# Modulation rows 2, 3 and 4 as half rows in column strips, loaded back repeated over the partitions

## The chip, the cores and the metric

One core of one Trainium2 chip runs the kernel. The metric is the device time of one execution in microseconds (us), the median of several runs. Engines are named as in the profile: PE (TensorE, matmuls), DVE (VectorE), ACT (ScalarE), POOL (GpSimd), SP (SyncE, which here only issues DMAs).

## What is computed

One transformer block in bf16, forward and all gradients (batch 1, S = 2048 tokens, D = 1024, F = 3584):

```
mod = (silu(c) @ w_mod)              # c (1,1024), w_mod (1024, 6*1024)
sa, ca, ga, sb, cb, gb = six rows of mod, 1024 each
h = layernorm(x) * (1 + ca) + sa
x = x + ga * irfft2(rfft2(h) * (w_r + 1j*w_i))
h = layernorm(x) * (1 + cb) + sb
y = layernorm(h)
out = x + gb * (gelu(y @ w1 + b1) @ w2 + b2)
# outputs: out, and by vjp of grad_out the gradients of
# x, w_r, w_i, w1, b1, w2, b2, c, w_mod
```

The six rows of mod are numbered 0 (sa), 1 (ca), 2 (ga), 3 (sb), 4 (cb), 5 (gb). This case is about rows 2, 3 and 4.

## The kernel before

**The modulation.** Every elementwise operation with a row of mod needs that row on all 128 partitions. The kernel gets this from TensorE: `u_b` holds silu(c) as 8 blocks of 128 contraction rows, each column repeated over 128 columns. With a block of `u_b` as weights, a matmul gives the same row in all 128 partitions of its PSUM tile. `mod_block(r, h)` makes half h (512 columns) of row r: a weight tile `wblk` of w_mod (128x8x512, 1 MB, L245, on SP's queue, a ring of three tiles), 8 matmuls of 128x512 (L253) accumulating in a PSUM bank, a copy to the row's place (L256, on DVE or ACT as the scheduler picks), and for rows 1 and 4 an addition of one (L258, DVE). The places are `MOD_DST`: `ga_row` for row 2, `sb_row` for row 3 (half of the tile `sb_saf`), `opcb_row` for row 4 (1 + cb). Rows 1, 5 and 0 are made at the start; rows 2, 3 and 4 later, six blocks called `late_mods`.

**Fillers.** grad_out * gb times the transpose of W2 is needed only by the backward of the MLP. `ph_part(fc, js)` makes one of its 28 blocks of 128 rows: 4 x 8 matmuls (L684) into PSUM tiles `pp`, copies to `pho` or `phr` (L691, L694, ACT or DVE), and a store to `d_ph` on POOL's queue. `load_w2t(fg)` fetches the transposed weights for two blocks (L301, SP's queue, two slots `wt`). Six of these blocks (`PH_EARLY`) stand ahead of the spectral mixer, with three late modulation blocks behind fc=3 and three behind fc=5; the other 22 are dealt by the scheduler into places where PE has nothing else.

**The mixer and the MLP.** A loop over four pieces of 512 tokens (lines 709 to 722) normalizes x (`ln_mix`, `norm_act`: L451, L454, L461 on ACT and statistics on DVE), multiplies by 1 + ca, and folds it twice (`fold_tok`, `fold_d`, all additions at L173 on DVE) into `fbuf`; the last addition, of `saf`, completes a piece. The transforms are matmuls: `pu` (L472), `pcs` (L505), on DVE the products with the spectral weights (`R`), `pv` (L565), `po` (L630) with copies at L635. `consume_fwd(i)` takes a finished piece: unfolds it, stores it to `d_A`, multiplies by `ga_row`, adds x, normalizes, multiplies by `opcb_row`, adds `sb_row`, normalizes again, and stores to `d_n3`. Then `z_block(b, g0, g1)` runs the first MLP product (L802, PSUM `pz`) with a bias copy on ACT (L805), the square and two sigmoids on ACT (L807, L811, L813) and products on DVE; `bo_pass` runs the second product (L853).

**Order.** The kernel is written in a tile framework: a list scheduler puts the instructions of each engine in order before the run, `tc.high_priority()` puts an instruction ahead of others that are ready, and `tc.issue_after(x)` keeps it behind x. On the chip every engine and every DMA queue then works in that fixed order. So an edit in one place can move copies between ACT and DVE and fillers between stages elsewhere.

Of the kernel before, what the change touches and what calls it, by code (L numbers as in the profile page):

```python
# [11 lines left out]
BF16 = mybir.dt.bfloat16  # L12
I32 = mybir.dt.int32
ACT = mybir.ActivationFunctionType
ALU = mybir.AluOpType
AX = mybir.AxisListType

P = 128
S = 2048
D = 1024  # L20
# [4 lines left out]
KH = D // 2  # L25
# [10 lines left out]
def kernel(  # L36
# [24 lines left out]
    nc = tc.nc  # L61
# [5 lines left out]
    dram = ctx.enter_context(tc.tile_pool(name="dram", bufs=1, space=bass.MemoryType.DRAM))  # L67
# [5 lines left out]
    def ps_s(name):  # L73
        return psum.tile([P, 512], FP32, tag="s", name=name)
# [18 lines left out]
    opca_row, ga_row, opcb_row, gb_row = (rows4[:, r, :] for r in range(4))  # L93
# [19 lines left out]
    d_SI = dram.tile([P, 2, 4, 512], BF16, name="d_SI")  # L113
    d_E = dram.tile([P, 2, 8, 256], BF16, name="d_E")
    d_gmod = dram.tile([6 * D], BF16, name="d_gmod")
    d_ph_v = d_ph.rearrange("(fc p) s -> p fc s", p=P)
    d_hh_v = d_hh.rearrange("(fc p) s -> p fc s", p=P)
    d_gz_v = d_gz.rearrange("(fc p) s -> p fc s", p=P)
# [50 lines left out]
    def bcn(row, n):  # L169
        return bass.AP(tensor=row.tensor, offset=row.offset, ap=[row.ap[0], [0, n], row.ap[1]])  # L170

    def tt(out, a, b, op):
        return nc.vector.tensor_tensor(out=out, in0=a, in1=b, op=op)  # L173
# [56 lines left out]
    u_b = small.tile([P, NDC, P], BF16, name="u_b", tag="gmrow", bufs=1)  # L230
# [5 lines left out]
    MOD_DST = {0: sar[:, 0, 0, :], 1: opca_row, 2: ga_row, 3: sb_row, 4: opcb_row, 5: gb_row}  # L236
    wring = [0]

    def mod_tile():
        wring[0] += 1  # L240
        return reg.tile([P, NDC, KH], BF16, name="wblk", tag=PXT[3 + wring[0] % 3])

    def mod_load(r, h, wblk, eng):
        cb = 2 * r + h
        eng.dma_start(out=wblk, in_=w_mod[:, cb * KH:(cb + 1) * KH].rearrange("(j p) n -> p j n", p=P))  # L245

    def mod_block(r, h, wblk=None):
        if wblk is None:
            wblk = mod_tile()[:]
            mod_load(r, h, wblk, nc.sync)  # L250
        pm = ps_s("pm")
        for jc in range(NDC):
            nc.tensor.matmul(pm[:], lhsT=u_b[:, jc, :], rhs=wblk[:, jc, :], start=(jc == 0), stop=(jc == NDC - 1))  # L253
        dst = MOD_DST[r][:, h * KH:(h + 1) * KH]
        with tc.high_priority():
            nc.any.tensor_copy(out=dst, in_=pm[:])  # L256
        if r in (1, 4):
            nc.vector.tensor_scalar(out=dst, in0=dst, scalar1=1.0, scalar2=None, op0=ALU.add)  # L258

    def fold_d(dst, src, tmp):  # L260
        n = src.shape[1]
        fwd = src.rearrange("p c (b w) -> p c b w", w=512)[:, :, :, 0:256]
        rev = bass.AP(tensor=src.tensor, offset=src.offset + 1023, ap=[src.ap[0], [D, n], [-512, 2], [-1, 256]])
        tv = tmp.rearrange("p c (s b w) -> p c s b w", s=2, w=256)
        tt(tv[:, :, 0], fwd, rev, ALU.add)
        tt(tv[:, :, 1], fwd, rev, ALU.subtract)
        dv = dst.rearrange("p c (a b w) -> p c a b w", b=2, w=256)
        tt(dv[:, :, :, 0, :], tv[:, :, :, 0, :], tv[:, :, :, 1, :], ALU.add)
        return tt(dv[:, :, :, 1, :], tv[:, :, :, 0, :], tv[:, :, :, 1, :], ALU.subtract)
# [30 lines left out]
    def load_w2t(fg):  # L300
        w2t_in[0] = nc.sync.dma_start_transpose(out=wt[:, fg % 2], in_=B_w2[fg * 256:(fg + 1) * 256, :])  # L301
# [19 lines left out]
    for h in range(2):  # L321
        mod_block(1, h, wm[1, h][:])
# [17 lines left out]
    for j in range(4):  # L340
        for cch in range(NDC):
# [3 lines left out]
            if cch % 2 == 0:  # L345
                with tc.high_priority():
                    nc.vector.tensor_scalar(out=gBoT[j][:, cch, :], in0=pt[:], scalar1=gb_col[:, cch:cch + 1], scalar2=0.0,
                                            op0=ALU.mult, op1=ALU.add, accum_out=gu[:, j, cch:cch + 1])
# [68 lines left out]
    def ln_act(x4, row, i, jk):  # L417
        sv = small.tile([P, 4, 4], FP32, tag="lnsv")
        for q in range(4):
            nc.scalar.activation(out=jk[:, q, :], in_=x4[:, q, :], func=ACT.Identity, accum_out=sv[:, q, 0:1])  # L420
        nc.vector.tensor_scalar(out=sv[:, :, 1:2], in0=sv[:, :, 0:1], scalar1=-1.0 / D, scalar2=None, op0=ALU.mult)
        for q in range(4):
            nc.scalar.activation(out=jk[:, q, :], in_=x4[:, q, :], func=ACT.Square, bias=sv[:, q, 1:2], accum_out=sv[:, q, 2:3])
        ln_fin(sv[:, :, 2:3], sv[:, :, 1:2], sv[:, :, 3:4], 1.0 / D, row, i)
# [7 lines left out]
    def ln_dve(x4, row, i):  # L432
        st = small.tile([P, 4, 2, nc.vector.BN_STATS_DIM], FP32, tag="lnst", bufs=1)
        mv = small.tile([P, 4, 4], FP32, tag="lnmv")
        for q in range(4):
            for h in range(2):
                nc.vector.bn_stats(out=st[:, q, h, :], in_=x4[:, q, h * KH:(h + 1) * KH])
            nc.vector.bn_aggr(out=mv[:, q, 0:2], in_=st[:, q])
        nc.vector.tensor_scalar(out=mv[:, :, 2:3], in0=mv[:, :, 0:1], scalar1=-1.0, scalar2=None, op0=ALU.mult)
        ln_fin(mv[:, :, 1:2], mv[:, :, 2:3], mv[:, :, 3:4], 1.0, row, i)  # L440

    def ln_mix(x4, row, i, jk):
        st = small.tile([P, 4, 2, nc.vector.BN_STATS_DIM], FP32, tag="lnst", bufs=1)
        mv = small.tile([P, 4, 4], FP32, tag="lnmv")
        for q in range(2):
            for h in range(2):
                nc.vector.bn_stats(out=st[:, q, h, :], in_=x4[:, q, h * KH:(h + 1) * KH])
            nc.vector.bn_aggr(out=mv[:, q, 0:2], in_=st[:, q])
        nc.vector.tensor_scalar(out=mv[:, 0:2, 2:3], in0=mv[:, 0:2, 0:1], scalar1=-1.0, scalar2=None, op0=ALU.mult)
        for q in range(2, 4):  # L450
            nc.scalar.activation(out=jk[:, q, :], in_=x4[:, q, :], func=ACT.Identity, accum_out=mv[:, q, 0:1])  # L451
        nc.vector.tensor_scalar(out=mv[:, 2:4, 2:3], in0=mv[:, 2:4, 0:1], scalar1=-1.0 / D, scalar2=None, op0=ALU.mult)
        for q in range(2, 4):
            nc.scalar.activation(out=jk[:, q, :], in_=x4[:, q, :], func=ACT.Square, bias=mv[:, q, 2:3], accum_out=mv[:, q, 0:1])  # L454
        nc.vector.tensor_scalar(out=mv[:, 2:4, 1:2], in0=mv[:, 2:4, 0:1], scalar1=1.0 / D, scalar2=None, op0=ALU.mult)
        ln_fin(mv[:, :, 1:2], mv[:, :, 2:3], mv[:, :, 3:4], 1.0, row, i)
# [216 lines left out]
    last_pe = [None]  # L673
# [4 lines left out]
    def ph_part(fc, js):  # L678
        fg, k = fc // 2, fc % 2
        ph2 = phs[fc % 4]  # L680
        for j in js:
            pp = ps_f("pp")
            for cch in range(NDC):
                last_pe[0] = nc.tensor.matmul(pp[:], lhsT=wt[:, fg % 2, cch, k * P:(k + 1) * P], rhs=gBoT[j][:, cch, :],  # L684
                                              start=(cch == 0), stop=(cch == NDC - 1))
            q = (0, 2, 3, 1)[j]
            ov = ph2[:, :, q * P:(q + 1) * P]
            pv = pp[:, :].rearrange("p (i w) -> p i w", w=P)
            if j % 2 == 0:
                with tc.high_priority():  # L690
                    nc.any.tensor_copy(out=ov, in_=pv)  # L691
            else:
                with tc.high_priority():
                    nc.any.tensor_copy(out=ov, in_=bass.AP(tensor=pv.tensor, offset=pv.offset + 511, ap=[pv.ap[0], [-P, 4], [-1, P]]))  # L694
        if js[-1] == 3:
            nc.gpsimd.dma_start(out=d_ph[fc * P:(fc + 1) * P, :], in_=ph2.rearrange("p i w -> p (i w)"))

    PH_EARLY = 6
    late_mods = [(r, h) for r in (2, 3, 4) for h in range(2)]
    for fc in range(PH_EARLY):  # L700
        ph_part(fc, (0, 1, 2, 3))
        if fc % 2 == 1:
            load_w2t(fc // 2 + 2)
            if fc > 1:
                with tc.issue_after(last_pe[0].ins):
                    for r, h in late_mods[3 * (fc // 2 - 1):3 * (fc // 2)]:
                        mod_block(r, h)

    for i in range(4):
        x4, fb = x4s[i], fbuf[:, i]  # L710
        if i == 0:
            with tc.issue_after(u_in.ins):
                ln_dve(x4, 0, i)
        elif i > 0:
            ln_mix(x4, 0, i, fb)
        else:
            ln_act(x4, 0, i, fb)
        norm_act(fb, x4, 0, i)
        tt(fb, fb, bcn(opca_row, 4), ALU.mult)
        fold_tok(fb, x4)  # L720
        fold_d(fb, fb, x4[:])
        tt(fb[:, 0, :], fb[:, 0, :], saf, ALU.add)
    css = reg.tile([P, 2, 2, 2 * PW], BF16, name="cs01", tag="px0")
    nc.gpsimd.memset(css[:], 0.0)

# [206 lines left out]
    for g in range(7):  # L932
        wtile = reg.tile([P, 4, D], BF16, name=f"w1T_{g}", tag=W1T[g])
        for k in range(4):
            fc = g * 4 + k
# [162 lines left out]
    for b in range(NB):  # L1098
# [42 lines left out]
        for i in range(4):  # L1141
            t = 4 * b + i
            nc.vector.tensor_tensor_reduce(out=g2[:, i, :], in0=gn3[:, i, :], in1=opcb_row, scale=1.0, scalar=0.0,
                                           op0=ALU.mult, op1=ALU.add, accum_out=s2c[:, i:i + 1])
# [222 lines left out]
```

## Time and profile before

| | before |
|---|---|
| runs (us) | 1461.4, 1461.49, 1465.73; median 1461.49 |
| profiled execution (us) | 1459.13, span of the trace 1457.3 |
| granted PE clock, mean | 0.992 |
| busy | PE 96%, DVE 73%, ACT 52%, POOL 25% |
| L253, all 96 matmuls of the six rows | 27.9 us busy |

A line of a timeline has the start in us, the busy time in us, the engine, the source line, the operation with its tiles, the count of instructions taken together, and in brackets the idle time of the engine before it with what ended that. A group line has busy us and mean ns, then the idle time before the group's instructions and its main releaser. A matmul's own duration (379 ns) overlaps its neighbours'; the spacing, 0.217 us for 128x512, is what counts. In a line of windows the last three columns are the granted PE clock, the DMA share and GB/s.

### The profile page before, as it was taken

The numbers are of one execution on the slowest core, as the hardware profiler recorded it, in microseconds if no ns is written. First come the engines' busy times: TensorE is split into PE (matmuls) and PEld (weight loads), VectorE is DVE, ScalarE is ACT, GpSimd is POOL, SyncE is SP. The second block draws the span as 40 slices with busy tenths as digits, with TensorE's granted clock in tenths as the row PEclk, the third lists the DMA queues.
The fourth block names the chain that finished last, engine by engine and source line by source line (L and its number), as shares of the span: only waits on it lengthen the run. The fifth ranks groups of instructions, "written<-read, shape, count | busy, mean of one in ns | idle before, by whom it ended". The sixth has DMA issues, their size and how long they took to land. (4 is left out here: it accounts for less than half of the span.)

```text
span 1457.3 us, 18411 instructions
## 1 busy us (share of the span) xinstructions
PE 1396.5 (96%) x6835; PEld 649.0 (45%) x6835; DVE 1058.4 (73%) x1483; ACT 752.2 (52%) x1065; POOL 366.1 (25%) x441
## 2 busy tenths in 40 slices
PE   5889999999999999999999999999999999999997
PEld 2434545444444444444444444344444445444443
DVE  5884786898799787887520889898467678898650
ACT  4675555857887766665305574342622434344211
POOL 6520451211112122122211011021245441222432
PEclk8999999999999999999999999999999999999999
DMA  9962473899887877697998275297699987766991
GB/s 333 286 214 70 142 235 115 270 255 337 257 203 278 259 250 233 201 264 241 277 297 245 74 271 185 107 270 176 181 217 254 254 233 213 194 191 180 297 279 65
DMA packets 358367, 324.28 MB, mean 223 GB/s; under 512 B 209386, under 2 KB 301056, under 8 KB 358022
## 3 DMA queue, kind: packets, MB, share of 16 engines
q1 hardware_dynamic: 324166, 207.71, 52.7%
q0 software_dynamic: 34112, 115.41, 22.6%
q8 instruction: 53, 0.87, 0.2%
q14 instruction: 36, 0.29, 0.1%
HBM read 162.06 MB, written 111.20 MB: 188 GB/s over the span
## 5 line engine op out<-in xcount | busy, mean ns | idle before, releaser
L684 PE MATMUL pp<-gBoT,wt 128*128 128x512 bf16 x896 | 197.9, 380 | 4.5 <-DMA wt<-in_B_w_dram 2.6
L950 PE MATMUL pg<-w1T,gzr 128*128 128x512 bf16 x896 | 197.1, 381 | 0.2 <-ACT gn3b L961 0.2
L1266 PE MATMUL gw1acc<-gzh,n3n 128*128 128x512 bf16 x896 | 195.4, 379 | 1.3 <-DMA gzh<-d_gz 1.3
L684 PEld LDWEIGHTS <-wt 128*128 128x128 bf16 x896 | 87.7, 98 | 109.4 <-issue 4.2
L950 PEld LDWEIGHTS <-gzr 128*128 128x128 bf16 x896 | 87.3, 98 | 108.7 <-issue 6.6
L802 PEld LDWEIGHTS <-w 128*128 128x128 bf16 x896 | 87.3, 98 | 108.8 <-issue 4.7
L1266 PEld LDWEIGHTS <-n3n 128*128 128x128 bf16 x896 | 87.4, 98 | 106.1 <-issue 2.7
L802 PE MATMUL pz<-n3Tb,w 128*128 128x512 bf16 x448 | 99.2, 379 | 1.6 <-DVE w2sD L875 1.4
L802 PE MATMUL pz<-n3Ta,w 128*128 128x512 bf16 x448 | 98.7, 379 | 1.1 <-ACT gt L805 1.1
L1075 PE MATMUL gw2acc<-gB,hhsA 128*128 128x512 bf16 x448 | 98.5, 379 | 1.0 <-DMA hhsA<-d_hh 1.0
L853 PEld LDWEIGHTS <-hhA 128*128 128x128 bf16 x608 | 59.0, 98 | 71.7 <-issue 1.4
L805 ACT ACTIVATE gt<-pz,b_col 128x512 bf16<-128x512 f32 x112 | 72.5, 684 | 34.2 <-PE pz L802 32.8
L1270 ACT CAST gwo<-gw1acc 128x512 bf16<-128x512 f32 x50 | 29.1, 583 | 113.6 <-PE gw1acc L1266 99.0
L173 DVE TENSOR_TENSOR gt<-gt,gt 128x2048 bf16<-128x2048 bf16 x56 | 68.3, 1223 | 22.4 <-ACT gt L813 21.2
L1082 ACT CAST gwo<-gw2acc 128x512 bf16<-128x512 f32 x46 | 26.7, 583 | 109.9 <-PE gw2acc L1075 75.6
L811 ACT ACTIVATE gt<-gt 128x2048 bf16<-128x2048 bf16 x28 | 53.5, 1910 | 55.7 <-DVE gt L173 55.7
L173 DVE TENSOR_TENSOR ct<-ct 128x2048 bf16<-128x2048 bf16 x64 | 75.9, 1218 | 1.8 <-DMA d_n<-ct 1.1
L1075 PEld LDWEIGHTS <-hhsA 128*128 128x128 bf16 x448 | 43.6, 98 | 53.0 <-DMA hhsA<-d_hh 1.7
L997 DVE CUSTOM_DVE_ANT_0 otl<-otl 128x1024 bf16<-128x1024 bf16 x24 | 29.1, 1223 | 49.9 <-DMA otl<-in_w_mod_dram 44.2
L807 ACT ACTIVATE gt<-gt 128x2048 bf16<-128x2048 bf16 x28 | 53.4, 1908 | 5.4 <-DVE hhC L173 2.5
L813 ACT ACTIVATE gt<-gt 128x2048 bf16<-128x2048 bf16 x28 | 53.5, 1909 | 0.5
L1271 POOL DMA_DIRECT2D out_dram<-gwo x56 | 30.6, 548 | 85.6 <-ACT gwo L1270 53.4
(325 smaller groups left out, 2531.5 us busy)
## 6 DMA issues: line engine op xcount, KB each, us to landing
gzr<-d_gz SPq DMA_DIRECT2D x28, 512.0 KB
wblk<-in_w_mod_dram SPq DMA_DIRECT2D x12, 1024.0 KB
out_dram<-otl POOLq DMA_DIRECT2D x48, 256.0 KB
out_dram<-gwo POOLq DMA_DIRECT2D x96, 128.0 KB
d_ph<-pho POOLq DMA_DIRECT2D x21, 512.0 KB
d_hh<-hhA POOLq DMA_DIRECT2D x19, 512.0 KB
w2sD<-in_B_w_dram SPq DMA_DIRECT2D x14, 512.0 KB
hhC<-d_ph SPq DMA_DIRECT2D x14, 512.0 KB
```

The source lines that it names most:

```text
L173: return nc.vector.tensor_tensor(out=out, in0=a, in1=b, op=op)
L684: last_pe[0] = nc.tensor.matmul(pp[:], lhsT=wt[:, fg % 2, cch, k * P:(k + 1) * P], rhs=gBoT[j][:, cch, :], start=(cch == 0), stop=(cch == ...
L802: last_pe[0] = nc.tensor.matmul(pz[:], lhsT=w1s[g][:, cch, k * P:(k + 1) * P], rhs=n3T[:, cch, :], start=(cch == 0), stop=(cch == NDC - 1))
L805: nc.scalar.activation(out=zb[:, k, :], in_=pz[:], func=ACT.Identity, bias=b1_col[:, fc:fc + 1], scale=1.0)
L807: nc.scalar.activation(out=av, in_=zb, func=ACT.Square)
L811: nc.scalar.activation(out=sg, in_=bv, func=ACT.Sigmoid, scale=2.0 * GK)
L813: nc.scalar.activation(out=bv, in_=bv, func=ACT.Sigmoid, scale=-2.0 * GK)
L853: last_pe[0] = nc.tensor.matmul(pbs[i][:], lhsT=hh[:, k, i * P:(i + 1) * P], rhs=wp[:, k, :], start=False, stop=(g == 6 and k == 3))
L950: last_pg[0] = nc.tensor.matmul(pgs[i][:], lhsT=gzs[b, g][:, k, i * P:(i + 1) * P], rhs=w1Ts[g][:, k, h * KH:(h + 1) * KH], start=(g == 0 ...
L1075: nc.tensor.matmul(acc[:], lhsT=hh_of(fc)[:, t, :], rhs=gBs[t // 4][:, t % 4, h * KH:(h + 1) * KH], start=(t == 0), stop=(t == NT - 1))
L1266: nc.tensor.matmul(acc[:], lhsT=n3ns[t // 4][:, t % 4, cch * P:(cch + 1) * P], rhs=gz2[t // 8][:, t % 8, :], start=(t == 0), stop=(t == NT ...
L1271: nc.gpsimd.dma_start(out=out_4[cch * P:(cch + 1) * P, fg * 512:(fg + 1) * 512], in_=ob)
```

## The change

A new generator `mod_strips(rows, stage)` takes the place of `mod_block` for rows 2, 3 and 4.

- The weights of a matmul are 32 columns of `u_b`, so one matmul fills a strip of 32 partitions of one PSUM tile `pm4`. Half h of the k-th row goes into strip 2k + h: rows 3 and 4 together fill four strips, row 2 alone two.
- A weight tile holds half of the contraction for a full row (128x4x1024, still 1 MB, still six of them in the same ring).
- For rows 3 and 4 the first half of the contraction is put behind fc=3 and the second behind fc=4, 16 matmuls each; both halves of row 2 are put behind fc=5.
- One copy on ACT brings the strips to the first half of `opcb_row` (rows 3 and 4) or of `ga_row` (row 2), used as a stage; DVE adds one to the strips of row 4; POOL's queue stores one partition of each strip to a new DRAM row `d_mod`, six stores of 1 KB.
- Behind the loop over the four pieces, three loads on SP's queue read the rows 3, 4 and 2 from `d_mod` into `MOD_DST`, repeated over all 128 partitions (256 KB each).

The scheduler's order also changes elsewhere. On PE, 99 matmuls of L684 stand between the last late modulation matmul and the `pu` matmuls that need the last piece of `fbuf`, where 69 stood; fewer stand in later stages. On SP the loads of `wt` for the 13th pair of blocks stand ahead of a store of `d_n`, not behind it. On DVE and ACT some copies (L635, L691, L694) change sides. Line numbers in the changed kernel are about 29 higher from the MLP on.

```diff
@@ -113,6 +113,7 @@
     d_SI = dram.tile([P, 2, 4, 512], BF16, name="d_SI")
     d_E = dram.tile([P, 2, 8, 256], BF16, name="d_E")
     d_gmod = dram.tile([6 * D], BF16, name="d_gmod")
+    d_mod = dram.tile([6 * D], BF16, name="d_mod")
     d_ph_v = d_ph.rearrange("(fc p) s -> p fc s", p=P)
     d_hh_v = d_hh.rearrange("(fc p) s -> p fc s", p=P)
     d_gz_v = d_gz.rearrange("(fc p) s -> p fc s", p=P)
@@ -256,6 +257,34 @@
             nc.any.tensor_copy(out=dst, in_=pm[:])
         if r in (1, 4):
             nc.vector.tensor_scalar(out=dst, in0=dst, scalar1=1.0, scalar2=None, op0=ALU.add)
+
+    def mod_strips(rows, stage):
+        pm = ps_s("pm4")
+        for jh in range(2):
+            wbs = []
+            for r in rows:
+                wb = mod_tile()[:].rearrange("p j n -> p (j n)").rearrange("p (j n) -> p j n", n=D)
+                nc.sync.dma_start(out=wb, in_=w_mod[jh * KH:(jh + 1) * KH, r * D:(r + 1) * D].rearrange("(j p) n -> p j n", p=P))
+                wbs.append(wb)
+            for jc in range(4):
+                for k in range(len(rows)):
+                    for h in range(2):
+                        s = 32 * (2 * k + h)
+                        nc.tensor.matmul(pm[s:s + 32, :], lhsT=u_b[:, 4 * jh + jc, 0:32], rhs=wbs[k][:, jc, h * KH:(h + 1) * KH],
+                                         start=(jh == 0 and jc == 0), stop=(jh == 1 and jc == 3))
+            if jh == 0:
+                yield
+        n = 64 * len(rows)
+        with tc.high_priority():
+            nc.scalar.copy(out=stage[0:n, :], in_=pm[0:n, :])
+        for k, r in enumerate(rows):
+            if r == 4:
+                nc.vector.tensor_scalar(out=stage[64 * k:64 * k + 64, :], in0=stage[64 * k:64 * k + 64, :], scalar1=1.0, scalar2=None,
+                                        op0=ALU.add)
+            for h in range(2):
+                s = 64 * k + 32 * h
+                nc.gpsimd.dma_start(out=d_mod[r * D + h * KH:r * D + (h + 1) * KH].rearrange("(o n) -> o n", o=1), in_=stage[s:s + 1, :])
+        yield
 
     def fold_d(dst, src, tmp):
         n = src.shape[1]
@@ -696,15 +725,16 @@
             nc.gpsimd.dma_start(out=d_ph[fc * P:(fc + 1) * P, :], in_=ph2.rearrange("p i w -> p (i w)"))
 
     PH_EARLY = 6
-    late_mods = [(r, h) for r in (2, 3, 4) for h in range(2)]
+    late_mods = {3: mod_strips((3, 4), opcb_row[:, 0:KH]), 5: mod_strips((2,), ga_row[:, 0:KH])}
+    late_mods[4] = late_mods[3]
     for fc in range(PH_EARLY):
         ph_part(fc, (0, 1, 2, 3))
         if fc % 2 == 1:
             load_w2t(fc // 2 + 2)
-            if fc > 1:
-                with tc.issue_after(last_pe[0].ins):
-                    for r, h in late_mods[3 * (fc // 2 - 1):3 * (fc // 2)]:
-                        mod_block(r, h)
+        if fc in late_mods:
+            with tc.issue_after(last_pe[0].ins):
+                for _ in range(2 if fc == 5 else 1):
+                    next(late_mods[fc])
 
     for i in range(4):
         x4, fb = x4s[i], fbuf[:, i]
@@ -720,6 +750,8 @@
         fold_tok(fb, x4)
         fold_d(fb, fb, x4[:])
         tt(fb[:, 0, :], fb[:, 0, :], saf, ALU.add)
+    for r in (3, 4, 2):
+        nc.sync.dma_start(out=MOD_DST[r], in_=d_mod[r * D:(r + 1) * D].partition_broadcast(P))
     css = reg.tile([P, 2, 2, 2 * PW], BF16, name="cs01", tag="px0")
     nc.gpsimd.memset(css[:], 0.0)
```

## The prediction

> **What bounds the kernel now.** I read the page first, then TensorE's timeline around the six late blocks of the modulation, then the column strips that the kernel already has elsewhere, and last, stage by stage, which engine releases TensorE. The page:
>
> ```profile
> PE 1396.5 (96%) x6835; PEld 649.0 (45%) x6835; DVE 1058.4 (73%) x1483; ACT 752.2 (52%) x1065; POOL 366.1 (25%) x441
> L684 PE MATMUL pp<-gBoT,wt 128*128 128x512 bf16 x896 | 197.9, 380 | 4.5 <-DMA wt<-in_B_w_dram 2.6
> ```
>
> TensorE is busy 96%, so taking matmuls away looks like time. But the 896 matmuls of L684 (197.9 us, 0.22 each) are filler: they need nothing from the spectral mixer and lie wherever TensorE would otherwise wait for it. Time saved among fillers moves filler forward; it shortens the program only if the next work is released earlier too. TensorE around the late blocks (start, busy, idle before it and who ended that):
>
> ```profile
> 81.81 3.62 PE L253 MATMUL pm<-wblk,u_b 128*128 128x512 bf16 x16
> 88.89 2.83 PE L253 MATMUL pm<-wblk,u_b 128*128 128x512 bf16 x8 [3.46 <-DVE rows L256]
> 91.52 14.76 PE L684 MATMUL pp<-gBoT,wt 128*128 128x512 bf16 x64
> 106.12 5.34 PE L253 MATMUL pm<-wblk,u_b 128*128 128x512 bf16 x24
> ...
> 112.89 14.84 PE L684 MATMUL pp<-gBoT,wt 128*128 128x512 bf16 x68
> 128.32 0.60 PE L472 MATMUL pu<-smA,fbuf 128*128 128x512 bf16 x2 [0.60 <-DVE fbuf L173]
> ```
>
> The 48 matmuls take 81.81 to 91.52 and 106.12 to 111.4, 15.1 us in all: 48 x 0.217 = 10.4 of work, 3.46 of waiting for a PSUM bank, the rest a slow clock after it. And the gate is seen: at 128.32 TensorE waits for VectorE's last folded piece. VectorE has no idle over 2.1 us from 84.69 to 128.27 and does not depend on TensorE's fillers. Further on:
>
> ```profile
> 330.05 13.99 PE L684 MATMUL pp<-gBoT,wt 128*128 128x512 bf16 x64 [2.62 <-DMA wt<-in_B_w_dram]
> 343.87 7.07 PE L802 MATMUL pz<-n3Ta,w 128*128 128x512 bf16 x32
> ...
> 400.84 4.48 PE L802 MATMUL pz<-n3Ta,w 128*128 128x512 bf16 x20 [1.12 <-ACT gt L805]
> ```
>
> The fillers end here; the z matmuls (L802) begin at 343.87, and at 400.84 TensorE waits for ScalarE. After that its longest wait up to 467 is under 0.2 us. So the clock of this case is the release at 400.84, and ScalarE sets it:
>
> ```profile
> 396.50 1.91 ACT L811 ACTIVATE gt<-gt 128x2048 bf16<-128x2048 bf16 x1 [3.63 <-DVE gt L173]
> 398.32 1.89 ACT L807 ACTIVATE gt<-gt 128x2048 bf16<-128x2048 bf16 x1
> 400.12 2.40 ACT L805 ACTIVATE gt<-pz,b_col 128x512 bf16<-128x512 f32 x4
> ```
>
> Windows of the stages before it (length, then busy time of TensorE, its loads, VectorE, ScalarE, GpSimd):
>
> ```profile
> 89.00:92.00 3.00, 3.00 (x10) 1.10 (x9) 3.00 (x2) 2.42 (x5) 0.00 (x0) 0.61 0.98 318
> 92.00:93.00 1.00, 1.00 (x4) 0.40 (x3) 1.00 (x2) 1.00 (x2) 0.00 (x0) 0.50 1.03 409
> ...
> 300.00:342.00 42.00, 39.38 (x184) 17.69 (x182) 41.40 (x54) 24.45 (x37) 5.43 (x9) 1.00 0.92 255
> 345.00:391.00 46.00, 46.00 (x217) 20.68 (x216) 30.95 (x54) 41.91 (x47) 6.82 (x9) 1.00 0.94 317
> ```
>
> From 300 to 342 VectorE is full (41.40 of 42), from 345 to 391 ScalarE (41.91 of 46): TensorE is not what sets 400.84.
>
> **The change, part by part.** *The matmuls.* Still 48, now 32 columns wide. The column sums of the backward already run as such strips (L196):
>
> ```profile
> 1034.51 0.61 PE L196 MATMUL acc3b<-au,ones_bf 128*32 128x512 bf16 x8
> 1035.06 1.25 PE L472 MATMUL pu<-smB,fbuf 128*128 128x512 bf16 x5
> ```
>
> Eight strips take 0.55 us from start to start, sixteen at 820.45 take 0.97 up to the next work: four strips side by side cost one pass of 0.217, and a stretch has 0.11 besides. Rows 3 and 4 have four strips and two stretches of sixteen: 1.94. Row 2 alone has two, so eight passes: 8 x 0.217 + 0.11 = 1.85. Together 3.8 against 15.1: TensorE is 11.3 us shorter here. The bank wait goes, since one bank serves two rows and no copy stands between.
>
> *Loads.* Six tiles of 1 MB as before, but each holds half the contraction. The second tiles of rows 3 and 4 are needed at fc=4, about 89.7; in the trace three tiles issued at 83.98 to 92 landed near 89, 93.6 and 97.7. I take 1 us of waiting, bounds 0 and 4 (the third landing's 97.7 is for row 2). It lies ahead of the gate: nothing on the path.
>
> *Copies.* Six of L256 (0.58 on ScalarE, 0.69 on VectorE) become two, two L258 (0.29) become one on 64 partitions. VectorE loses 2 x 0.69 + 0.29 = 1.7 in its chain to 128.3. Against it the fold's order moves, and one more cast stands ahead; I take the gate 0.4 later, bounds -1.7 and +1.5.
>
> *Store and load back.* Six stores of 1 KB are queued on GpSimd ahead of d_ph stores, three broadcast loads of 256 KB on SyncE. Each load waits for a store that waits for the copy, and the transposes of fg4 and fg5 (L301) stand behind them on SyncE. In the trace fg4 was issued at 106.31. Its readers now come about 64 fillers after 101, at 116, against some 8.2 us (two such transposes held SyncE's queue 16.45 us from 314.91), so it is covered; without that cover each microsecond is one of idle, with another 4 us to the gate. The rows are read from 238 on (ga) and 268 (1+cb): over 100 us of cover.
>
> *Fillers.* On TensorE 99 of L684 now stand before the gate, not 69: 30 x 0.2165 = 6.5 us. In the mixer's later stages the fillers are dealt anew, and after its last group of po, 294 remain where 316 did: 4.8 us. The 2.62 wait at 330.05 goes too: fg12's transpose was issued at 314.91 behind a store of d_n, and now stands ahead of it. So TensorE reaches z some 4.8 + 2.6 = 7.4 us early, near 336.5.
>
> *What that is worth at 400.84.* Three terms. (a) VectorE's stage of pair products (57.47 busy of 62 us) loses two casts, 2 x 0.66 = 1.3; with the gate's +0.4, -0.9. (b) From the last products to the add of the fourth consumed piece VectorE now has 28 casts (15 of po at L635, 13 of L691 and L694), before 24 (9 and 15): 4 x 0.69 = 2.75 more. VectorE idled 8.3 of 112 us from 230 to 342; between 0 and 2.75 I take the half, +1.4. (c) Three L805 of the first z (0.67 each) now stand ahead of L451 of the fourth piece, in time that ScalarE had idle before 341.36, and so leave its full stretch: -2.0, bounds 0 and -2.7. Sum -0.9 + 1.4 - 2.0 = **-1.5 us**. TensorE's lead of 7.4 becomes 5.9 us of waiting ahead of z(0,5).
>
> That waiting has a price of its own. After 3.46 us of idle the clock was 0.61 and then 0.50 (windows above, some 3.4 us long); 2.78 at 915.42 was also followed by 0.50, while 2.62 at 330.05 was not (1.00). At half clock 3.4 us lose 1.7. The Trainium skill, "TensorE: Matmul & The Clock Gate", Part 1, says the clock falls to half after at least one idle window of about 3.4 us, windows running free of the program; the 2.78 here is shorter than that and enough. By that rule the 5.9 us, if they came in one piece, would cost 1.7 and the sum would be +0.2. I do not add it, since z(0,0) to z(0,4) wait for the same ScalarE chain and should take the idle in pieces.
>
> The profiled execution was 1459.13 (span 1457.3), 2.36 under the median of 1461.49; I take the difference to the median: 1461.49 - 1.5 = **1460.0**. A measurement of this kernel tells about 0.3% from no change, 4.4 us.
>
> **Rivals.** *A, the lead is carried through.* If z(0,0) to z(0,3), finished 7.4 us earlier, let ScalarE run its square and sigmoids in its idle time (3.63 at 396.50 and the 1.0s before), the release moves with TensorE: -7.4, 1454.1. For it: VectorE idled 7.96 us before 391.11 for ScalarE. Against: ScalarE's 41.91 of 46. Chance 0.22.
>
> *B, slower: VectorE's queue behind the po copies.* In the second consumed piece VectorE does the last six L635, ScalarE did seven of eight before; the tile is free only when a store of d_A has landed, for which ScalarE waited 1.56 at 270.28 and 0.72 at 251.74. VectorE works in order, so the multiply by 1+cb, LN2 of the first piece and everything behind would wait. All of the 2.75 plus 2.28, less the 0.9: +4.1; TensorE's lead and this make an idle of 11 us, above the 3.46 that halved the clock: +1.7. 1467.3. It decides if the store lands over 2 us after VectorE gets there. Against it: VectorE is itself late here. Chance 0.20.
>
> *C, the strips do not run side by side* with real weights of their own: 48 x 0.217 stay, only the bank wait and cold clock go; 4.7 us less filler time, TensorE's lead near 1, and 400.84 barely moves: 1460.5 to 1461.5. Against it the 0.55 for eight. Chance 0.06.
>
> **How the numbers follow.** Forecast 0.52, its own range 1457.5 to 1464.0 from the bounds of (b) and (c). Faster by over 0.3%: A and a rest, 0.26; slower: B and a rest, 0.22; within 0.52. The range runs 1453.5 to 1467.0, to A below and to just short of B above.
>
> **What would show it.** Right: strips of 0.97 and 1.9 us; the first fold gate within 1 us of 128.3; z from about 336; then idle on TensorE in front of L802 released by ScalarE's L805, 4 to 7 us in sum before 401; L635 with six copies on VectorE at 270. Wrong: z(0,5) before 396 (A), VectorE waiting for a d_A store (B), strips spaced 0.217 (C), or a wait for wt between 110 and 128.

## The result, and the profile after

| | before | changed |
|---|---|---|
| median of 6 runs (us) | 1462.61 (1459.19 to 1469.21) | 1481.91 (1478.13 to 1489.74) |
| profiled execution, span (us) | 1459.13, 1457.3 | 1478.26, 1476.0 |
| granted PE clock, mean | 0.992 | 0.986 |

The ratio is 1.0131 [1.0095, 1.0168]: slower by 19 us, with 14 to 25 inside the interval. The prediction was "no change", 1460.0, with 1467.0 as its upper end. It missed in sign and in range. Ratios go by the fast runs alone and are not quotients of the medians shown; one run of e7 below (1508.88, granted clock 0.938) was slow and counts in its median only.

The page of the changed kernel, the engines and the filler group:

```profile
PE 1391.1 (94%) x6704; PEld 647.3 (44%) x6835; DVE 1058.9 (72%) x1483; ACT 749.4 (51%) x1060; POOL 372.1 (25%) x447
L713 PE MATMUL pp<-gBoT,wt 128*128 128x512 bf16 x874 | 197.0, 381 | 6.9 <-DMA wt<-in_B_w_dram 3.8
```

TensorE's busy time reads 5.4 us less (1396.5 before), but 131 of its 6835 matmul records are missing in this trace, which leaves 6.7 us of gaps under 0.07 us (0.4 before), so it is in truth about the same. VectorE has 0.5 us more and GpSimd 6.0. TensorE's gaps of 0.07 us and more grew from 50.6 to 67.6 us: the loss is waiting. L713 is the old L684; its longest wait, for `wt`, was 2.6 and is 3.8. TensorE's timeline at the places of the prediction, with the same columns as there:

```profile
81.35 1.05 PE L273 MATMUL pm<-wblk,u_b 128*32 128x512 bf16 x16
...
90.54 1.04 PE L273 MATMUL pm<-wblk,u_b 128*32 128x512 bf16 x14 [0.80 <-DMA wblk<-in_w_mod_dram]
98.52 1.90 PE L273 MATMUL pm<-wblk,u_b 128*32 128x512 bf16 x16
...
129.20 0.38 PE L501 MATMUL pu<-smA,fbuf 128*128 128x512 bf16 x1 [0.79 <-DVE fbuf L174]
...
198.33 8.61 PE L594 MATMUL pv<-smi,R 128*128 128x512 bf16 x32 [3.94 <-ACT V L676]
...
336.54 7.08 PE L713 MATMUL pp<-gBoT,wt 128*128 128x512 bf16 x31 [3.75 <-DMA wt<-in_B_w_dram]
343.46 7.07 PE L834 MATMUL pz<-n3Ta,w 128*128 128x512 bf16 x32
...
406.45 8.66 PE L834 MATMUL pz<-n3Ta,w 128*128 128x512 bf16 x32 [4.97 <-ACT gt L837]
```

The strips are as forecast, and the gate (129.20, was 128.32) too. Then two things are new: a wait of 3.94 in the middle of `pv`, where before none stood, and a longer idle, 4.97 in one piece ahead of z(0,5), which is released at 406.45 instead of 400.84 (another 2.01 stands ahead of z(0,4), at 390.96). Each of the two is followed by 32 matmuls in some 8.6 us where 7.07 is usual; behind the 3.75 for `wt` the clock stayed at 1.00. A window behind the second (length, busy time of TensorE, its loads, VectorE, ScalarE, GpSimd, then granted clock, DMA share, GB/s):

```profile
406.00:410.00 4.00, 3.55 (x10) 1.25 (x10) 2.77 (x4) 4.00 (x6) 0.32 (x1) 0.57 0.85 269
```

The clock is 0.57 there. The next work, at 407.74 before, starts at 414.94: 7.2 us late. Of this 1.6 is given back by 469, since the kernel before has a wait some way on that the changed one has not (TensorE's timeline of before):

```profile
467.47 1.89 PE L802 MATMUL pz<-n3Tb,w 128*128 128x512 bf16 x8 [1.39 <-DVE w2sD L875]
```

So at 469 the difference is 5.6 again, and the slow clock behind z(0,5) has cost nothing in the end. From z(0,5) on TensorE has the same order in both kernels; on the other queues a few neighbours change places up to 477, and behind that every queue has the same order. The traces then differ by 8.3 us at 1034, 17.8 at 1128 and 18.0 at 1305. What stands at 469 is the work of the new order; what the later 12 are is weighed below.

**Where the 3.94 comes from.** SyncE's, GpSimd's, VectorE's and ScalarE's timelines of the changed kernel, in this order:

```profile
174.46 2.91 SPq L330 DMA_TRANSPOSE wt<-in_B_w_dram  x1
```
```profile
182.89 6.32 POOL L520 DMA_INDIRECT ws<-in_A_w_r_dram,xu  x1 [0.30 <-issue]
```
```profile
191.67 1.23 DVE L174 TENSOR_TENSOR qa<-Pt,ws 128x2052 bf16<-128x2052 bf16 x1 [3.33 <-issue]
193.37 1.23 DVE L174 TENSOR_TENSOR qb<-Pt,ws 128x2052 bf16<-128x2052 bf16 x1 [0.46 <-DMA ws<-in_A_w_i_dram,xu]
```
```profile
197.10 0.73 ACT L676 CAST cs<-pcs 128x512 bf16<-128x512 f32 x1 [3.82 <-DVE qb L174]
```

The `wt` transposes for the seventh pair of filler blocks (fg6, L330, old L301) are issued at 174.46; before they stood at 181.30, behind the loads of `ws` of the fifth step. GpSimd's gather of `ws` takes 6.32 us where the same gather took 2.06 before:

```profile
183.02 2.06 POOL L491 DMA_INDIRECT ws<-in_A_w_r_dram,xu  x1 [0.30 <-issue]
```

VectorE's products read what it brings. VectorE began the last sums of the previous `R` at 187.05, 2.2 us earlier than before (1.45 of that is a wait for `ws` that stood there before and is gone), and then stood idle for 3.33 and 0.46. The profile names no releaser for the 3.33; e1 below shows that it goes with the long gather. ScalarE holds a copy of `pcs` that waits 3.82 us for those products, and the copies of `V` that TensorE needs stand behind it in its queue. So one transfer's place on SyncE went through four engines. `po` starts 3.4 us late (234.08, was 230.71).

**In the consume stage** VectorE's timeline shows the mechanism of rival B:

```profile
269.79 2.29 DVE L174 TENSOR_TENSOR xt<-ct,xt 128x4096 bf16<-128x4096 bf16 x1
272.00 0.68 DVE L723 CAST pho<-pp 128x512 bf16<-128x512 f32 x1
273.37 1.89 DVE L664 CAST ct<-po 128x512 bf16<-128x512 f32 x3 [0.69 <-DMA d_A<-ct]
275.51 1.89 DVE L664 CAST ct<-po 128x512 bf16<-128x512 f32 x3 [0.25 <-PE po L659]
277.32 2.28 DVE L174 TENSOR_TENSOR ct<-ct,rows 128x4096 bf16<-128x4096 bf16 x1
```

The last line is the multiply by 1 + cb of the first piece. Before it started 3.37 us after the add of x (265.38 to 268.75), here 7.53: six copies of `po` (L664) with 0.94 of waiting stand between, 4.2 us. One of them stood just behind that multiply before (271.55), which gives 1.1 back: the delay against before grows from 4.4 us at the multiply by ga to 8.6 here, and is 7.5 at the next step.

**ScalarE at z(0,0)**:

```profile
347.11 0.69 ACT L837 ACTIVATE gt<-pz,b_col 128x512 bf16<-128x512 f32 x1 [1.04 <-PE pz L834]
348.84 0.69 ACT L837 ACTIVATE gt<-pz,b_col 128x512 bf16<-128x512 f32 x1 [1.04 <-PE pz L834]
349.43 1.05 ACT L480 ACTIVATE ct<-xt 128x1024 bf16<-128x1024 bf16 x1
```

The last line begins the fourth piece's statistics. The add that feeds them is 6.5 us late (345.51, was 338.99), they are 8.1 late (349.43, was 341.36), because three bias copies (L837) ahead of them wait for z, and z itself was not early.

### The profile page after: what moved, and what is told of

Its sections match the earlier page's. It is cut to its first block, busy times and chain, and to the rows that moved or that the text cites. A ratio compares the mean times of both kernels' runs of the same rounds, so it can differ in the third digit from the quotient of the medians.

```text
span 1476.0 us, 18286 instructions
## 1 busy us (share of the span) xinstructions
PE 1391.1 (94%) x6704; PEld 647.3 (44%) x6835; DVE 1058.9 (72%) x1483; ACT 749.4 (51%) x1060; POOL 372.1 (25%) x447
## 5 line engine op out<-in xcount | busy, mean ns | idle before, releaser
L713 PE MATMUL pp<-gBoT,wt 128*128 128x512 bf16 x874 | 197.0, 381 | 6.9 <-DMA wt<-in_B_w_dram 3.8
L713 PEld LDWEIGHTS <-wt 128*128 128x128 bf16 x896 | 87.6, 98 | 111.3 <-issue 5.6
L837 ACT ACTIVATE gt<-pz,b_col 128x512 bf16<-128x512 f32 x112 | 72.3, 684 | 37.0 <-PE pz L834 34.7
```

Source lines behind the costliest of these rows:

```text
L837: nc.scalar.activation(out=zb[:, k, :], in_=pz[:], func=ACT.Identity, bias=b1_col[:, fc:fc + 1], scale=1.0)
```

## The experiments

Ratios are against the kernel before on the same chip, medians in us. If nothing else is said, an edit is made to the changed kernel; of each edit the lines that decide are shown, and lines that only keep a reference to an instruction are left out. Where a stage is given, it runs from the gate to z(0,5): 272.5 before (400.84 - 128.32), 277.3 in the changed kernel (406.45 - 129.20).

### The place of fg6's transposes, the copies of po, the new DRAM row

**e1_pin** moves one SyncE instruction behind the loads of the fifth `ws` pair, nothing else.

```diff
-            load_w2t(fc // 2)
+            with tc.issue_after(ws_ld[4].ins) if fc == 12 else ExitStack():
+                load_w2t(fc // 2)
```

> The changed kernel with one instruction moved: SyncE's transposes of wt for fg6 go behind the fifth pair of ws loads, as in the kernel before, not ahead of it. Theory 1 (the order of that one load makes GpSimd's gathers of the spectral weights late): the gather of ws_r that took 6.32 us takes about 2, VectorE's wait of 3.33 + 0.46 before the sixth pair product goes, TensorE's 3.94 at 198 and the slow clock behind it go, the first po is near 230 instead of 234.1, and the program is 3 to 5 us faster than the changed kernel: about 1474 to 1476 in profile, ratio to before 1.008 to 1.011. Rival (the stores and loads of d_mod or their place in DRAM cost the time everywhere): the gather stays slow or the gain is lost by 340, ratio 1.013 as for the changed kernel.

**e2_po** puts seven of the last eight copies of `po` on ScalarE; **e3_pin_po** does both.

```diff
+                        if fwd and i == 3 and (cl, hh_) != (1, 1):
+                            nc.scalar.copy(out=ov, in_=po[:])
-                        if fwd or (cl, hh_) != (3, 0):
+                        elif fwd or (cl, hh_) != (3, 0):
```

> The changed kernel with seven of the last piece's eight po copies fixed on ScalarE (one on VectorE), as the scheduler had it before; some copies behind them change sides too. Theory 2 (VectorE's queue behind the po copies, rival B): the multiply by 1+cb of the first piece, 277.3 in the changed kernel, comes about 3 to 4 us earlier, z(0,5) is released 2 to 4 us earlier than 406.4, and the program is 2 to 5 us faster than the changed kernel, ratio 1.010. Rival (ScalarE's chain alone sets 406): no gain, since ScalarE gets 3 us more work.

> Both edits. If the two causes are separate, the gains add: z(0,5) near 400 or earlier, 6 to 9 us faster than the changed kernel, ratio 1.005 to 1.008; what is left would be the backward, some 9 us in the profiles. If one of them hides the other: about the better of the two alone.

**e4_no_new_dram** takes the old DRAM tile `d_gmod` for the six stores and three loads (`d_mod = d_gmod`). Its instruction order is that of the changed kernel on every engine.

> The changed kernel with the rows kept in the existing DRAM row of gradients (d_gmod, written again only in the backward) instead of a new DRAM tile d_mod; the order of instructions on all engines is that of the changed kernel. If the new tile moves later DRAM buffers and this costs the 9 us that the backward lost: ratio about 1.007. If not: 1.013 as the changed kernel, the forward gates at 198 and 406 unchanged in either case.

| | median | ratio |
|---|---|---|
| e1_pin | 1477.48 | 1.0083 [1.0051, 1.0114] |
| e2_po | 1492.79 | 1.0173 [1.0137, 1.0208] |
| e3_pin_po | 1482.99 | 1.0104 [1.0071, 1.0136] |
| e4_no_new_dram | 1485.94 | 1.0144 [1.0110, 1.0179] |

e4 is in effect a second look at the changed kernel, on the same chip as e1, and it agrees with 1.0131: the new DRAM tile is not the cause. e1 is 8.5 us below it, at intervals that just touch (against the changed kernel's own 1.0131 they overlap). GpSimd's gather and TensorE's `pv` in e1:

```profile
183.18 1.55 POOL L522 DMA_INDIRECT ws<-in_A_w_r_dram,xu  x1 [0.30 <-issue]
```
```profile
196.95 7.07 PE L598 MATMUL pv<-smi,R 128*128 128x512 bf16 x32 [0.75 <-ACT V L680]
```

1.55 instead of 6.32, 0.75 of waiting instead of 3.94, full clock, and `po` at 231.2. That this order made the gather long is shown: it took 6.32 or 6.33 in all four profiles with the transposes ahead of the `ws` loads (the changed kernel, e2, e4, e13) and 1.54 to 1.56 in all nine with them behind. e1's stage is 277.3, 4.5 shorter than e4's 281.8, but no shorter than in the changed kernel's first profile: z(0,5) is still 5.9 us late. That first profile was lucky with the clock. Behind its wait of 3.75 for `wt` 31 matmuls took 7.08; in e1 (3.78) they took 10.04, in e13 below (3.65) 9.88, so that z(0,0) came nearly 3 us later. The line of e13:

```profile
336.32 9.88 PE L715 MATMUL pp<-gBoT,wt 128*128 128x512 bf16 x31 [3.65 <-DMA wt<-in_B_w_dram]
```

And what came early at `po` met VectorE's six copies and ScalarE's three L837 again.

e2 is slower than the changed kernel, against what was expected. ScalarE's timeline in e2:

```profile
275.37 3.50 ACT L490 ACTIVATE ct<-xt,stats 128x1024 bf16<-128x1024 bf16 x3
278.82 1.07 ACT L664 CAST ct<-po 128x512 bf16<-128x512 f32 x2
280.20 2.76 ACT L664 CAST ct<-po 128x512 bf16<-128x512 f32 x5 [0.31 <-PE po L659]
282.86 1.24 ACT L490 ACTIVATE ct<-xt,stats 128x1024 bf16<-128x1024 bf16 x1
```

The scheduler put all seven copies ahead of the fourth normalization (L490) of the first piece, 4 us in the same chain, and z(0,5) came at 419.16 (of which 3.4 us is a gate at 132.55, explained below). This moved the wait to another engine and did not take it away, so e2 and e3 do not tell what the copies cost on VectorE.

### The copies and the bias copies in other places

**e6_pin_z** is e1 with the bias copies of z(0,0) kept behind the fourth piece's statistics. **e7_pin_po_order** is e1 with the seven copies on ScalarE behind the four normalizations. **e8_all_three** has both.

```diff
-                with tc.high_priority():
+                with tc.high_priority(), (tc.issue_after(sq_in[1, 3].ins) if n == 0 else ExitStack()):
```
```diff
+                        if fwd and i == 3 and (cl, hh_) != (1, 1):
+                            with tc.issue_after(na_in[1, 0].ins):
+                                nc.scalar.copy(out=ov, in_=po[:])
```

> e1 and the bias copies of z(0,0) on ScalarE kept behind the two sums of the fourth piece (first operation of ln_mix on ScalarE), as before, not three of them ahead. In e1 these waited for TensorE's z until 349 while the piece had been ready since 345: the statistics of the fourth piece went from +3.8 to +7.0 us there. Theory (ScalarE's queue blocked by the L805 put ahead): the fourth piece's statistics at about 353.5, z(0,5) 2 to 3 us earlier than the 406.8 of e1, ratio 1.006. Rival (the full ScalarE stretch sets it, and the order in it is worth nothing): no change from e1, 1.008.

> e1 and seven of the last eight po copies on ScalarE, but now behind the four normalizations of the first piece, as before; in e2 and e3 all seven stood ahead of one of these and made it late. Theory: the multiply by 1+cb of the first piece comes within 1.5 us of before (268.8), against +5.9 in e1; the chain to z(0,5) 3 to 4 us earlier than e1, ratio 1.006. If copies on ScalarE cost as much as on VectorE: +4 to +6 remains and the ratio is that of e1, 1.008.

> e7 and e6 together: all three orders as before. Theory: z(0,5) within 1.5 us of the 400.8 of before, ratio 1.003 to 1.005, the rest being the backward if that is systematic, 1.000 if it is not. Rival: TensorE's earlier fillers cost elsewhere and z(0,5) stays above 404.

| | median | ratio | gate, stage |
|---|---|---|---|
| e6_pin_z | 1476.05 | 1.0062 [1.0039, 1.0085] | 134.3, 273.2 |
| e7_pin_po_order | 1478.81 | 1.0076 [1.0043, 1.0109] | 130.8, 274.9 |
| e8_all_three | 1477.28 | 1.0074 [1.0047, 1.0102] | 134.5, 273.0 |

With the bias copies behind the statistics the stage is within 1 us of before. So (c) of the prediction had the wrong sign: in this order the three L837 cost up to 4 us (277.3 to 273.2). Not all of this need be theirs: the 31 matmuls behind the wait for `wt` took 10.04 in e1 and 8.47 in e6, and some instructions of VectorE and ScalarE around z(0,0) change places too. The copies of `po` are worth 2.4 at the most (277.3 to 274.9), and nothing more once the bias copies are moved. The times hardly fall, since in these profiles the gate itself is up to 6 us late. That was a new question: the gate was at 129.20 in the first profile of the changed kernel.

### The gate: row 4's second tile

e4, whose order is that of the changed kernel, shows it. TensorE, then VectorE, then TensorE at the gate:

```profile
96.90 1.89 PE L273 MATMUL pm<-wblk,u_b 128*32 128x512 bf16 x14 [7.75 <-DMA wblk<-in_w_mod_dram]
```
```profile
99.45 0.29 DVE L282 TENSOR_SCALAR rows<-rows 64x512 bf16<-64x512 bf16 x1 [3.25 <-ACT rows L279]
```
```profile
132.73 0.38 PE L501 MATMUL pu<-smA,fbuf 128*128 128x512 bf16 x1 [0.78 <-DVE fbuf L174]
```

Row 4's second tile lands late: it reuses the first tile's memory, free only when the first strips are done at 82.4, and it stands on SyncE behind fg3's transposes, which held that queue 2.92 us in one profile and 4.5 to 5.2 in others. The strips wait 7.75, the copy L279 waits for them, and VectorE waits 3.25 for the copy to add one (L282). That addition stands inside VectorE's chain of folds, so the gate comes 4.4 us late. Over eight profiles of kernels with this order the strips waited 0.80 to 9.65 us; up to 5.7 left the gate within 1.3 of before, 7.75 gave 132.73 and 9.65 gave 134.54. In the kernel before the blocks are needed later, and in five profiles with its order (before, e5, e11, e12, e15) the gate lay between 126.3 and 128.3.

**e9_late_tile** (e6, with the second half of rows 3 and 4 put behind fc=5 and the addition and the stores behind the folds) and **e10_add_late** (only the addition and the stores put there) take L282 out of the chain. **e13_tile_first** (alone) and **e14_all_orders** (with e6) load that tile ahead of fg3's transposes.

```diff
-        if fc % 2 == 1:
+        if fc % 2 == 1 and fc != 3:
             load_w2t(fc // 2 + 2)
...
+        if fc == 4:
+            with tc.issue_after(wb_in[0].ins):
+                load_w2t(3)
```

> e6, and the second half of the contraction of rows 3 and 4 behind fc=5, not fc=4, and the addition of one and the six stores behind the last addition of the fold. In e8's profile the second tiles landed at 99.4, TensorE waited 9.65 us at 89.7, and VectorE's addition of one (L282), in order in the middle of its fold, waited 5.14 us for the copy of these strips, so that the gate was at 134.5; in the changed kernel's profile the same wait was 0.80 and the gate 129.2. Theory (late tile and VectorE's queue): the gate is at 126.5 to 129.5, z(0,5) near 401, 3 to 6 us faster than e6: ratio 1.001 to 1.003. Rival (the rest of the loss lies behind 401): ratio as e6, 1.006.

> As e9, but the second half of rows 3 and 4 stays behind fc=4: only the addition and the stores leave VectorE's fold. If the wait in VectorE's queue alone sets the gate: as e9. If TensorE's own wait for the tile sets it too (99 fillers stand behind it ahead of the gate): in an execution with a late tile the gate is still near 133, and the ratio lies between e9's and e6's.

> The changed kernel with one instruction moved on SyncE: the second tile of row 4 is loaded ahead of the transposes of fg3, not behind them; the order of all else is as in the changed kernel. Theory (the tile is late because the transposes hold SyncE's queue, 2.9 to 5.2 us, and move 1 MB beside it): TensorE's wait for the tile at 89.7, 5.4 to 9.6 us in nine profiles, falls to 0 to 3, VectorE's wait in front of L282 goes, the gate is at 128 to 129.5, and the program is 2 to 5 us faster than the changed kernel: ratio 1.010. Rival (the tile is late because of the DMA load of that time, whatever the order): wait and gate as before, 1.013.

> e13 and e6 together: the tile of row 4 ahead of the transposes of fg3, the transposes of fg6 behind the fifth ws pair, and L805 of z(0,0) behind the sums of the fourth piece. If the three orders are the loss: the gate at 128 to 129.5, z(0,5) at 401 to 402, ratio 1.002 to 1.004, about that of the transfers alone (e5, 1.0028). If the rest lies behind 401: 1.006 as e6 and e9.

| | median | ratio | gate |
|---|---|---|---|
| e9_late_tile | 1475.56 | 1.0059 [1.0037, 1.0081] | 130.37 |
| e10_add_late | 1478.08 | 1.0067 [1.0044, 1.0090] | 130.99 |
| e13_tile_first | 1479.09 | 1.0091 [1.0070, 1.0111] | 127.26 |
| e14_all_orders | 1475.92 | 1.0079 [1.0051, 1.0107] | 127.53 |

e9 and e10 failed as a remedy: in e9 the tiles were still waited for (5.4 us in three pieces), and VectorE now waited 3.83 for a filler's result. In e10 the strips waited 7.26 and the gate was at 130.99, where 7.18 with L282 in the chain (e2) gave 132.55; VectorE now waited 3.54 for ScalarE's L486, which stood behind copies of fillers that TensorE had made late. So L282 is only one of the ways by which the late tile reaches the gate. e13 takes the wait itself away. Its strips and its gate on TensorE:

```profile
88.67 1.05 PE L275 MATMUL pm<-wblk,u_b 128*32 128x512 bf16 x16
...
127.26 0.38 PE L503 MATMUL pu<-smA,fbuf 128*128 128x512 bf16 x1 [1.03 <-DVE fbuf L174]
```

No wait, and a gate within the 126.3 to 128.3 of the old order, 5.5 us ahead of e4's; z(0,5) is 5.5 ahead of e4's too (409.04, was 414.54). One SyncE instruction moved takes the ratio from 1.0131 (or 1.0144) to 1.0091, about 6 us, at intervals that overlap (or touch). e14 has all three orders mended and z(0,5) at 402.10, 1.3 late, yet the time does not go back to that of before, and its ratio is no better than that of e6, which has the tile late. What stands ahead of z(0,5) in e14:

```profile
402.10 8.75 PE L846 MATMUL pz<-n3Ta,w 128*128 128x512 bf16 x32 [4.74 <-ACT gt L849]
```

TensorE arrives early and waits for ScalarE in one piece of 4.74; 32 matmuls then take 8.75. Work saved ahead of ScalarE's release has become idle. At 469 e14 is only 1.2 late (the slow clock is given back there too), against 5.6 in the first profile of the changed kernel and 14.1 in e4's. So up to 469 the three orders account for nearly the whole loss. The 10 us that are left in e14's median (1475.92 against 1465.79) come later.

### What the transfers cost by themselves

**e5_dma_only** adds the six stores and the three broadcast loads to the kernel *before*, every other instruction as it was; **e12_stores_only** the stores alone. **e11_before_again** is the kernel before, unchanged. **e15_three_loads** adds three tiny loads on SyncE to the kernel before, **e16_shift_sixteen** thirteen such loads to e14, to see whether what counts is the place in the queue.

```diff
+    for r in (3, 4, 2):
+        for h in range(2):
+            nc.gpsimd.dma_start(out=d_mod[r * D + h * KH:r * D + (h + 1) * KH].rearrange("(o n) -> o n", o=1), in_=MOD_DST[r][0:1, h * KH:(h + 1) * KH])
+        nc.sync.dma_start(out=MOD_DST[r], in_=d_mod[r * D:(r + 1) * D].partition_broadcast(P))
```

> The kernel before, plus only the six stores of rows 2, 3 and 4 to d_mod and the three broadcast loads back into the same places (the rows themselves are made as before); the order of all other instructions on all five engines is that of the kernel before. If the transfers or their place in the queues cost the time, the backward included (9 to 13 us in all profiles of changed kernels so far): ratio 1.006 or more, the backward from 1040 to 1230 that much longer. If only the order made by the shorter matmuls costs: ratio 1.000 within the interval, gates of the profile within 1 us of before up to 930.

> The kernel before, unchanged: what two sets of runs of one kernel differ by, and a second profile of its backward. All theories: ratio 1.000 within the interval. If the backward from 930 to 1290 varies by itself, its profile differs from the first by several us there, as the kernel with the transfers alone did (+14 in its slowest execution); if it is steady, within 1 us.

> The kernel before plus only the six stores of 1 KB on GpSimd's queue, without the three broadcast loads on SyncE's; the order of all else is as before. e5 (both) had 1.0028 [1.0013, 1.0044]. If the stores on GpSimd cost it: 1.003. If the broadcast loads do: 1.000.

> The kernel before plus three loads of 2 KB on SyncE (b2_row's partitions 0 to 2 read once more), at the place of the broadcast loads; the order of all else is as before. If the shift by three of the later transfers costs the backward its time: ratio 1.003 to 1.008 and a backward 5 us or more longer than e11's. If the number of transfers does not matter: 1.000, and what e5 lost (1.0028) is the broadcast loads' and stores' own.

> e14 plus thirteen such loads of 2 KB, so that later transfers on SyncE are shifted by sixteen against before, not by three. If the place in the queue matters: ratio 1.000 to 1.004, against e14's 1.008. If not: as e14 or, by the loads' own cost, a little slower.

| | median | ratio |
|---|---|---|
| e5_dma_only | 1470.32 | 1.0028 [1.0013, 1.0044] |
| e12_stores_only | 1469.87 | 1.0017 [0.9999, 1.0035] |
| e11_before_again | 1466.90 | 0.9994 [0.9973, 1.0015] |
| e15_three_loads | 1466.78 | 1.0009 [0.9987, 1.0032] |
| e16_shift_sixteen | 1473.91 | 1.0054 [1.0035, 1.0073] |

Stores and loads together cost about 4 us (2 to 6 by the interval), without any other change of order. The stores alone (e12) lie between and can be told from neither. That the place in SyncE's queue does it is not borne out: e15 cannot be told from the kernel before, nor quite from e5, and e16 lies a little below e14, at intervals that overlap. Nor is it a reader that waits for the rows: in its profile e5 is 1.6 us *early* at z(0,5), and loses its time after 469, hundreds of us after the last of these loads was issued (112.95); the profiled execution was the slowest of its twelve. e11's profile warns how far single profiles carry there: the unchanged kernel is 0.4 late at z(0,5) and 6.9 late at 1278 against its own first profile, which was a lucky one in the backward. From 1034 to 1305 profiles without the broadcast loads lose 0 to 7.9 us against that first one, the changed kernel and its variants 7.7 to 13.2, and e5 11.3.

**The sum.** By the ratios, out of 19 us, the late tile is worth about 6 (e13), fg6's place 7 (e1), and the bias copies 3 (e6 against e1, at intervals that overlap). They do not add: with all three mended 1.0054 to 1.0079 remains (e16, e14), 8 to 12 us, in their profiles nearly all of it behind 469 (e16 is 0.2 early there). The transfers by themselves give 4 of that kind (e5). Why transfers issued before 115 us, or a kernel that has them, should make the backward longer is open. The instruction order behind 477 is not it, since it is the same; the new DRAM row (e4) and the count of loads on SyncE (e15, e16) show no sign of it, though their intervals leave room for a few us. No version beats the kernel before.

## Why the prediction was wrong, step by step

- **The matmuls: right.** 1.05 and 1.90 us a stretch (0.97 and 1.85 forecast), side by side with weights of their own; C is out. The place too was right: TensorE was not what bound the stage.
- **Loads: this step failed, in size and in mechanism.** "I take 1 us of waiting, bounds 0 and 4 ... It lies ahead of the gate: nothing on the path." The first profile gave 0.80, the other seven with this order 5.4 to 9.65. The time of landing was read from three tiles of the old order, and the transposes ahead of the tile on SyncE were not counted. That the gate hides it is wrong: L282 brings the wait into VectorE's queue of folds, and late fillers bring it there through ScalarE (e10). "Does not depend on TensorE's fillers" was not so even in the trace of before, where VectorE waited 2.08 at 114.60 for a filler's result (L684).
- **Copies: right where the tile is in time.** Gate +0.9 in the first profile (+0.4 forecast, inside its bounds); -1.1 in e13, which the old order's own spread of 2 us covers.
- **Store and load back: nothing was priced, and about 4 us was measured** (e5). No reader waited for the rows, so the argument on cover was right; the cost lies elsewhere, after 469, and its cause is open.
- **Term (a): a saving eaten by a wait.** The chain of pair products came 2.2 us early at 187.05 (0.9 forecast; 1.45 of it is a wait for `ws` that went), and then waited 3.8 for the next `ws`. The order of SyncE was read only around fg4, fg5 and fg12; fg6's move ahead of `ws` was in the order and not weighed.
- **Term (b): +1.4 forecast, +4.2 measured at the multiply by 1 + cb, of which 1.1 came back at the next step.** This is B's mechanism, at 0.20, and close to its price. "VectorE is itself late here" covered only half: it reached the copies 0.69 before the store landed, below the 2 that B was to need, and the six copies themselves were the cost.
- **Term (c): -2.0 forecast, wrong in sign.** It rested on z at 336.5, in ScalarE's idle time. TensorE's lead of 7.4 was 0.4: 4.8 us fewer fillers were met by the 3.4 from `pv`, and the wait for `wt` did not go but grew from 2.62 to 3.75: fg12's transposes moved ahead of the store of `d_n` as forecast, but fg13's stayed behind it (issued at 325.91, the store at 321.15), and TensorE waited for those. The bias copies then waited 1.0 us each in ScalarE's full stretch.
- **The half clock was worked out and set aside.** "z(0,0) to z(0,4) ... should take the idle in pieces": 2.01 came ahead of z(0,4) and 4.97 in one piece ahead of z(0,5), the clock fell to 0.57, and 32 matmuls took 1.6 us more. The rule that the prediction cites (the Trainium skill, "TensorE: Matmul & The Clock Gate", Part 1) forecast that; the traces agree with it here, in e14 too. At z(0,5) it cost nothing in the end, since the wait of 1.39 at 467 took it up. Elsewhere it did cost: 1.5 us behind the 3.94 in `pv`, and in e1 and e13 nearly 3 behind the wait for `wt`, ahead of z. The length of the idle alone did not decide it: 3.75 in the first profile left the clock at 1.00, 2.16 at the same place in e5 was followed by 0.56.
- **A** fell with the lead. In e14 z(0,0) comes 2.4 us early and z(0,5) is released 1.3 late; but in e16, whose order is the same there, both come 2.4 earlier still. How far the release follows TensorE stays open.
- **The range.** The bounds of (b) and (c) alone give 1457.9 to 1463.3, a little less than the 1457.5 to 1464.0 stated; neither reaches 1481.9.

## What to carry to other kernels

Where a scheduler sets the order, a step that takes work off one engine also re-deals every queue; read the new order of each of them, the small instructions and the transfers above all, and ask for each what now stands behind it. A load whose memory is freed late, with other transfers ahead of it in an in-order queue, should be priced by its worst landing, and followed through the first instruction that waits for it inside a full chain. Work taken from an engine that waits for others further on comes back as idle there, here 4.7 us in one piece ahead of ScalarE's release.

## What the runs showed of the hardware that was not expected

- A GpSimd gather of `ws` took 6.32 or 6.33 us in four profiles where a `wt` transpose was issued on SyncE ahead of the `ws` loads, and 1.54 to 1.56 in nine where it stood behind them. What in the transfers holds it was not separated; another gather of `ws` shortly ahead takes some 6.2 us in every profile, that of before too.
- The same transfer order gives very different landings from one execution to the next: row 4's second tile was waited for from 0.80 to 9.65 us in eight profiles.
- How long TensorE stood idle did not decide alone whether the clock fell: at the wait for `wt` ahead of z, 2.16 us (e5) was followed by a clock of 0.56, 3.65 (e13) by 0.50, and 3.75 (the changed kernel) by 1.00.
- Two executions of one unchanged kernel differ by 6.8 us in a stretch of the backward with many transfers (1034 to 1305), so a single profile there tells nothing below that.
